# Polysketch attention and an ELU layer on one core: batch 1's attention output in products of 64 rows, its rows exchanged by DMA, and a new order around it

## The chip, the cores and the metric

The kernel runs on one core of a Trainium2 chip, and all seven inputs and the output lie in the chip's memory. The metric is the device time of one execution in microseconds (us), the lower the better. Engines are named as in the profile: PE is TensorE's matrix product and PEld its weight load, DVE is VectorE, ACT is ScalarE, POOL is GpSimd, and SP is the engine that here only issues DMA transfers. ACTq and SPq are the instructions with which ScalarE and SP issue transfers.

## The reference

Batch 4, 4 heads, sequence 1088, head dimension 32; the second part has 4352 tokens, 128 features and 2048 hidden units.

```
phi(x): a = S1 x, b = S2 x (8 values each); phi = outer(a, b), 64 features
kv  = sum over s of phi(k)[s, f] * v[s, d]         # per batch and head, 64 x 32
z   = sum over s of phi(k)[s, f]
att = (phi(q) kv) / (phi(q) z + 1e-6)              # seq x 32 per head
x   = att with the heads side by side              # 4352 x 128
h   = x @ w_in
g   = h if h > 0, else exp(min(h, 0)) - 1
out = g @ w_out
```

Inputs for q, k, v, the sketches S1, S2 and the two weight matrices are rounded to f32 on the chip where they come wider.

## The kernel before, in words

**Groups.** The 4352 tokens are worked in groups of 512 (numbers 0 to 7, two to a batch: groups 2 and 3 are batch 1, 4 and 5 batch 2, 6 and 7 batch 3) and one last group 8 of 256 that has the last 64 tokens of each batch. The hidden units are 8 column pairs `cp` of 2 x 128.

**The dense part of one group and one cp.** `mm1` (L910) makes h in two halves c, each 128 x 512 in a PSUM buffer named h, of which there are four; `elu_a` (L923) runs two ScalarE instructions (Relu, then Exp), `elu_d` (L934) one VectorE instruction that writes gg and frees the PSUM buffer; `sums7` (L791) forms on GpSimd, in three instructions, the sums that the seven-product scheme needs; `mm2_seven` (L819) adds seven block products of gg and of prepared weights (`weights7`, L783) into two accumulators in PSUM (pa and pb). At a group's end `fin_seven_copy`, `fin_seven_a`, `fin_seven_b`, `fin_seven_c` join the blocks and send the output rows by 16 transfers on SP's queue; `fin1` (L955) does so for group 0 with 8 transfers.

**The queries of a pair of groups.** `queries` (L751) takes two PSUM buffers named h and two named qps. With a group among its second argument it runs `q1` (L567), the sketch of the queries in products of 32 x 32; `q1_out` transposes the results, `q2_prod`, `q2_sum`, `q2_rec`, `q2_an` make the denominator and scale, `q2_half` (L694) forms the 64 features per token and head in two halves i, all on VectorE. `q4` (L702) brings the features onto the partitions, and `queries` with the group among its first argument makes the attention output x, which `q5_out` (ScalarE) copies to the tile xg that `mm1` reads.

**Two forms of the product for x.** A group named in `pairs` (L332: 4, 6 and 8) uses `q5_pairs` (L731): 16 products of 64 rows x 32 columns, in two rounds e, with the 64 features of a token on 64 partitions. VectorE's transpose works inside blocks of 32 partitions, so for these groups `q4` transposes into a tile qpF and then exchanges blocks of 32 partitions between the partitions by 8 DMA transfers per half i (two e, two u, two f), into `exch[i]` (L681), a part of the SBUF that held raw weights at the start. They go on SP's queue, but for two of group 4's half 0, on ScalarE's. A group not in `pairs`, before the change only group 2 (with 3), uses `q5` (L719): 32 products of 32 x 32, in two rounds f that add up in PSUM, straight from VectorE's transpose. Each product is two instructions in the profile.

**The key side.** `KF_late`, `KO_a`, `KO_b` and `KA` make phi(k) and kv of a batch, `Z` and `Z_share` its z. `KT_out` (L458) transposes kv and writes it to a scratch in memory (kvd), from which transfers on SP's queue read it back as the products want it: four copies into kvs for `q5` (batch 1 only), and into `kv2` (kvp in the profile) two halves f for each half of the partitions; the batches in `pair_b` fill both halves of the partitions, batch 1 before the change only its lower half, for group 8.

**What sets the order.** From L1297 on, the order is written out by hand, call by call, for all engines together. Each engine runs its own instructions in that order and waits by semaphores for what they need; nothing is moved between engines. A PSUM buffer or tile is taken again when its last reader is done. Up to `width[0] = 64` (L1620) the products of the dense part are made in blocks of 32 columns, after it in blocks of 64.

Of the kernel before, what the change touches and what calls it, by code (L numbers as in the profile page):

```python
# [29 lines left out]
def kernel(  # L30
# [24 lines left out]
    P = 128  # L55
# [646 lines left out]
    def q4(g, i=0):  # L702

        m = heads(g) * un[g]
        if g not in pairs:
            qpT[g, i] = work.tile([P, 4 * H, 2, 32], F32, name="qpT", tag="qpT", bufs=2)
            nc.vector.transpose(qpT[g, i][:, :m].rearrange("p m f s -> p (m f s)"),
                                qp.pop((g, i))[:, :m].rearrange("p m i j -> p (m i j)"))
            return
        t = work.tile([P, 2, 4 * H, 32], F32, name="qpF", tag="qpT", bufs=2)  # L710
        nc.vector.transpose(t[:, :, :m].rearrange("p f m s -> p m f s"),
                            qp.pop((g, i))[:, :m].rearrange("p m (f i) j -> p m f (i j)", f=2))
        to = qpT[g, i] = exch[i if g < NQ - 1 else 2]
        for e in range(2):
            for u in range(0, 4, 2):
                for f in range(2):
                    (nc.scalar if g == 4 and not i and e and f else nc.sync).dma_start(to[32 * (u + f):32 * (u + f) + 32, e, :m], t[32 * (u + e):32 * (u + e) + 32, f, :m])
# [579 lines left out]
    transp(kT, "k", 3, 9, NT)  # L1297
    queries((), (2,), (1, 4))
    mm1(1, 3, (0,))
    q1_out(2, (2,))  # L1300
    mm2(0, 7, True, (0,))
    q1_out(2, (1,))
    weights7(slice(4, 8), 0)
    elu_a(0, 7, 1, (1,))
    elu_d(0, 7, 1)
    q1_out(2, (3,))
    mm2(0, 7, True, (1,))
    mm1(1, 4, (1,))
    q1_out(2, (0,))
    q2_prod(2)  # L1310
    elu_a(1, 3, 0, (0,))
    elu_a(1, 3, 0, (1,))
    mm1(1, 3, (1,))
    elu_a(1, 3, 1, (0,))
    elu_d(1, 3, 0)
    fin1(0)
    q2_sum(2)
    sums7(1, 2, 1)
    weights7(slice(4, 8), 2)
    q2_rec(2)  # L1320
    elu_a(1, 4, 1, (0,))
    q2_an(2)
    mm1(1, 6, (1,))
    mm1(1, 4, (0,))
    elu_a(1, 3, 1, (1,))
    elu_d(1, 3, 1)
    elu_a(1, 4, 0, (0,))
    mm2_seven(1, 1, True, False)
    q2_half(2, 0)
    elu_a(1, 4, 0, (1,))  # L1330
    elu_d(1, 4, 0)
    weights7(slice(2, 4), 3)
    elu_a(1, 4, 1, (1,))
    elu_d(1, 4, 1)
    weights7(slice(2, 4), 2)
    weights7(slice(4, 8), 1)
    mm1(1, 6, (0,))
    elu_a(1, 6, 0, (0,))
    elu_a(1, 6, 1, (0,))
    elu_a(1, 6, 0, (1,))  # L1340
    elu_a(1, 6, 1, (1,))
    sums7(1, 2, 2)
    mm2_seven(1, 2, False, False)
    mm1(1, 5, (0,))
    mm1(1, 5, (1,))
    sums7(1, 3, 0)
    sums7(1, 3, 1)
    q2_half(2, 1)
    weights7(slice(4, 8), 3)
    elu_a(1, 5, 0, (0,))  # L1350
    elu_a(1, 5, 1, (0,))
    elu_a(1, 5, 1, (1,))
    elu_d(1, 6, 1)
    sums7(1, 3, 2)
    elu_d(1, 6, 0)
    sums7(1, 4, 0)
    weights7(slice(0, 1), 1)
    sums7(1, 4, 1)
    sums7(1, 4, 2)
    weights7(slice(0, 1), 3)  # L1360
    mm2_seven(1, 3, False, False)
    elu_a(1, 5, 0, (1,))
    q4(2, 0)
    elu_d(1, 5, 1)
    elu_d(1, 5, 0)
    sums7(1, 5, 0)
    mm1(1, 7, (1,))
    mm1(1, 7, (0,))
    sums7(1, 5, 1)
    sums7(1, 5, 2)  # L1370
    q4(2, 1)
    elu_a(1, 7, 0, (0,))
    elu_a(1, 7, 0, (1,))
    keep_last(0)
    sums7(1, 6, 0)
    sums7(1, 6, 1)
    mm2_seven(1, 4, False, False)
    queries((2,), (), (2, 0))
    elu_a(1, 7, 1, (0,))
    elu_a(1, 7, 1, (1,))  # L1380
    mm2_seven(1, 5, False, False)
    q5_out(2, 1, 1)
    q5_out(2, 0, 0)
    q5_out(2, 0, 1)
    mm1(2, 0, (0,))
    q5_out(2, 1, 0)
    elu_a(2, 0, 0, (0,))
    elu_a(2, 0, 0, (1,))
    elu_d(1, 7, 0)
    sums7(1, 6, 2)  # L1390
    elu_d(1, 7, 1)
    sums7(1, 7, 0)
    transp(kT, "k", 2, 9, NT)
    KF_late(2, None)
    KF_late(3, (2, 1))
    KF_late_out(3, 1)
    KF_late_out(2, 1)
    elu_d(2, 0, 0)
    KF_late_out(2, 0)
    KF_late_out(3, 0)  # L1400
    mm1(2, 0, (1,))
    keep_last(1)
    sums7(1, 7, 1)
    elu_a(2, 0, 1, (0,))
    elu_a(2, 0, 1, (1,))
    KO_a(2, 0)
    elu_d(2, 0, 1)
    mm2_seven(1, 6, False, False)
    mm1(2, 1, (1,))
    KO_b(2, 0)  # L1410
    sums7(1, 7, 2)
    mm2_seven(1, 7, False, True)
    elu_a(2, 1, 1, (0,))
    mm1(2, 1, (0,))
    sums7(2, 0, 0)
    KO_a(2, 1)
    fin_seven_copy(1)
    KO_b(2, 1)
    mm1(2, 2, (1,))
    mm1(2, 2, (0,))  # L1420
    KA(2, (0,))
    sums7(2, 0, 1)
    elu_a(2, 1, 1, (1,))
    elu_d(2, 1, 1)
    fin_seven_a(1, 3)
    fin_seven_a(1, 0)
    fin_seven_a(1, 1)
    fin_seven_b(1, 0)
    fin_seven_a(1, 2)
    elu_a(2, 1, 0, (0,))  # L1430
    elu_a(2, 1, 0, (1,))
    elu_d(2, 1, 0)
    sums7(2, 1, 0)
    KA(2, (1,))
# [12 lines left out]
    fin_seven_b(1, 1)
    elu_d(2, 2, 1)
    sums7(2, 2, 0)
    mm1(2, 3, (1,))  # L1450
    elu_a(2, 3, 0, (1,))
    elu_a(2, 3, 1, (0,))
    zls[2] = ZC(2, kv_ps[2])
    KO_b(3, 0)
    mm2_seven(2, 0, True, False)
    elu_d(2, 3, 0)
    elu_a(2, 3, 1, (1,))
    elu_d(2, 3, 1)
    KO_a(3, 1)
    KO_b(3, 1)  # L1460
    Z(2, kv_ps[2], zls[2])
    mm1(2, 4, (0,))
    mm1(2, 5, (0,))
    sums7(2, 1, 1)
    elu_a(2, 4, 1, (0,))
    sums7(2, 1, 2)
    mm2_seven(2, 1, False, False)
    elu_a(2, 5, 0, (0,))
    elu_a(2, 4, 0, (0,))
    elu_a(2, 4, 1, (1,))  # L1470
    elu_d(2, 4, 1)
    sums7(2, 2, 1)
    sums7(2, 2, 2)
    mm1(2, 5, (1,))
    elu_a(2, 4, 0, (1,))
    elu_a(2, 5, 0, (1,))
    mm2_seven(2, 2, False, False)
    transp(qT, "q", 2, 0, 9)
    sums7(2, 3, 0)
    elu_d(2, 4, 0)  # L1480
    Z_out(2, kv_ps[2])
    fin_seven_c(1)
    transp(qT, "q", 3, 0, 9)
    elu_a(2, 5, 1, (0,))
    mm1(2, 6, (0,))
    KA(3, (0,))
    elu_a(2, 5, 1, (1,))
    elu_d(2, 5, 1)
    transp(qT, "q", 2, 9, NT)
    mm1(3, 0, (0,))  # L1490
    KA(3, (1,))
    elu_a(3, 0, 0, (0,))
    elu_a(3, 0, 0, (1,))
    mm1(3, 0, (1,))
    elu_d(2, 5, 0)
    mm1(2, 6, (1,))
    sums7(2, 3, 1)
    zls[3] = ZC(3, kv_ps[3])
    sums7(2, 3, 2)
    mm2_seven(2, 3, False, False)  # L1500
    elu_a(3, 0, 1, (0,))
    KT_out(3)
    Z(3, kv_ps[3], zls[3])
    sums7(2, 4, 0)
    sums7(2, 4, 1)
    sums7(2, 5, 0)
    sums7(2, 5, 1)
    Z_share(2)
    sums7(2, 4, 2)
    mm2_seven(2, 4, False, False)  # L1510
    elu_a(3, 0, 1, (1,))
    elu_d(3, 0, 0)
    Z_out(3, kv_ps[3])
    elu_d(3, 0, 1)
    sums7(3, 0, 0)
    sums7(2, 5, 2)
    mm1(2, 7, (0,))
    elu_a(2, 6, 0, (0,))
    elu_a(2, 6, 1, (0,))
    elu_a(2, 6, 0, (1,))  # L1520
    elu_d(2, 6, 0)
    elu_a(2, 6, 1, (1,))
    elu_d(2, 6, 1)
    transp(qT, "q", 3, 9, NT)
    Z_share(3)
    mm1(2, 7, (1,))
    elu_a(2, 7, 0, (0,))
    mm2_seven(2, 5, False, False)
    elu_a(2, 7, 1, (0,))
    elu_a(2, 7, 0, (1,))  # L1530
    elu_d(2, 7, 0)
    sums7(2, 6, 0)
    queries((), (4, 8), (3, 1))
    mm1(3, 2, (1,))
    elu_a(2, 7, 1, (1,))
    elu_d(2, 7, 1)
    elu_a(3, 2, 1, (0,))
    q1_out(4, (3,))
    elu_a(3, 2, 1, (1,))
    sums7(2, 6, 1)  # L1540
    mm1(3, 2, (0,))
    sums7(2, 6, 2)
    sums7(2, 7, 0)
    sums7(2, 7, 1)
    q1_out(4, (2,))
    elu_a(3, 2, 0, (0,))
    elu_a(3, 2, 0, (1,))
    mm2_seven(2, 6, False, False)
    q1_out(4, (0,))
    q1_out(4, (1,))  # L1550
    q1_out(8, (2,))
    q2_prod(4)
    q1_out(8, (1,))
    mm1(3, 1, (1,))
    sums7(2, 7, 2)
    mm2_seven(2, 7, False, True)
    q1_out(8, (0,))
    q2_sum(4)
    q2_rec(4)
    elu_d(3, 2, 1)  # L1560
    q2_an(4)
    q2_a(4, 1)
    elu_a(3, 1, 1, (0,))
    elu_d(3, 2, 0)
    sums7(3, 2, 0)
    mm1(3, 1, (0,))
    q2_half(4, 1)
    elu_a(3, 1, 1, (1,))
    elu_d(3, 1, 1)
    mm1(3, 4, (0,))  # L1570
    q4(4, 1)
    elu_a(3, 1, 0, (0,))
    elu_a(3, 1, 0, (1,))
    elu_d(3, 1, 0)
    mm1(3, 3, (0,))
    fin_seven_copy(2)
    fin_seven_a(2, 1)
    elu_a(3, 3, 0, (0,))
    fin_seven_a(2, 0)
    fin_seven_b(2, 0)  # L1580
    sums7(3, 0, 1)
    sums7(3, 0, 2)
    fin_seven_b(2, 1)
    fin_seven_b(2, 2)
    elu_a(3, 3, 0, (1,))
    mm1(3, 3, (1,))
    q2_a(4, 0)
    q2_half(4, 0)
    elu_a(3, 4, 0, (0,))
    sums7(3, 2, 1)  # L1590
    mm1(3, 4, (1,))
    sums7(3, 1, 0)
    mm2_seven(3, 0, True, False)
    sums7(3, 1, 1)
    elu_a(3, 4, 0, (1,))
    elu_d(3, 4, 0)
    sums7(3, 1, 2)
    elu_a(3, 4, 1, (0,))
    elu_a(3, 4, 1, (1,))
    elu_a(3, 3, 1, (0,))  # L1600
    elu_a(3, 3, 1, (1,))
    q4(4, 0)
    sums7(3, 2, 2)
    mm2_seven(3, 1, False, False)
    mm2_seven(3, 2, False, False)
    mm1(3, 5, (1,))
    elu_d(3, 4, 1)
    sums7(3, 4, 0)
    elu_d(3, 3, 0)
    q1_out(8, (3,))  # L1610
    elu_d(3, 3, 1)
    sums7(3, 3, 0)
    elu_a(3, 5, 1, (0,))
    elu_a(3, 5, 1, (1,))
    mm1(3, 5, (0,))
    elu_a(3, 5, 0, (0,))
    elu_a(3, 5, 0, (1,))
    elu_d(3, 5, 1)
# [355 lines left out]
```

## Time and profile before

| what | value |
|---|---|
| median of 3 runs | 259.54 us (258.89 to 260.28) |
| the profiled execution | 260.47 us, of which its span is 258.3 us |
| granted TensorE clock, mean | 0.997 of full |
| transfers | 16.56 MB in 30907 packets, mean 64 GB/s |
| first product of the reordered stretch (L1298's q1) starts | 52.85 us |
| product of groups 2 and 3 (L1378) starts | 70.06 us |
| sketch of the queries of groups 4, 5 and 8 (L1533) starts | 104.62 us |
| product of groups 4 and 5 (L1630) starts | 125.53 us |

How to read it: the page gives the busy time of each engine and its share of the span; the chain of work that ended last follows the end of the kernel back through what released each step; the timeline lists one engine's instructions by start and duration. Starts of PE in the timeline lie a few hundredths before those in the chain, since a product overlaps the one before it; the chain's pieces add up without overlap. A DMA issue is an instruction of SPq or ACTq; the transfer lands later, and the view of a tile gives both times.

### The profile page before, as it was taken

How to read it: one execution, taken by the hardware profiler on the slowest of the kernel's cores; microseconds unless marked ns; L12 is line 12 of the kernel's file. 1: busy time of each engine (PE TensorE's matmuls, PEld its weight loads, DVE VectorE, ACT ScalarE, POOL GpSimd, SP SyncE). 2: the span in 40 equal slices, each digit the busy share in tenths (PEclk: the TensorE clock that was granted, in tenths of full speed). 3: DMA queues.
4: the chain of work that ended last, by engine and by line, in shares of the span. 5: the costliest groups of instructions: out<-in, count | busy, mean ns of one | idle time of the engine just before them, and what ended most of it. 6: DMA issues, size and time to landing. Idle time of an engine off the chain costs nothing.

```text
span 258.3 us, 9778 instructions
## 1 busy us (share of the span) xinstructions
PE 251.8 (97%) x4101; PEld 159.8 (62%) x4101; DVE 174.6 (68%) x342; ACT 182.0 (70%) x357; POOL 184.1 (71%) x236
## 2 busy tenths in 40 slices
PE   8789999999999999999999999999999999999994
PEld 7653333426666677657648466666766666667994
DVE  5898998898859875797658587743455445644651
ACT  2589887748757657676577877578677777777792
POOL 5433365698994978877858887987888888888310
PEclk9999999999999999999999999999999999999998
DMA  6999593313000011114102004312021100110021
GB/s 178 303 366 238 177 285 65 95 23 55 7 5 4 15 18 27 25 35 105 35 13 31 0 7 94 83 39 33 11 32 28 19 3 0 24 20 3 3 33 31
DMA packets 30907, 16.56 MB, mean 64 GB/s; under 512 B 22512, under 2 KB 28016, under 8 KB 30864
## 3 DMA queue, kind: packets, MB, share of 16 engines
q1 hardware_dynamic: 29904, 15.04, 24.4%
q10 hardware_dynamic: 896, 0.84, 1.3%
q8 instruction: 32, 0.52, 0.9%
q14 instruction: 11, 0.09, 0.1%
q0 software_dynamic: 64, 0.07, 0.1%
HBM read 11.21 MB, written 2.36 MB: 53 GB/s over the span
## 4 chain that ended last, share of the span: by engine, by line
PE 94%; DMA 3%; ACTq 1%; ACT 0%; issue 0%; DVE 0%; DVEq 0%
PE h L259 46%; PE pb L839 18%; PE pa L839 15%; PE o L259 5%; PE ol L259 3%; DMA v<-in_v_dram 3%; PE kv L453 1%; PE qtp L640 1%; PE h L738 1%; PE h L574 1%; PE pb L815 1%; PE xps L666 1%; PE kv L439 1%; PE kfps L366 1%; ACTq L81 0%; PE h L726 0%
## 5 line engine op out<-in xcount | busy, mean ns | idle before, releaser
L938 DVE SCALAR_TENSOR_TENSOR gg<-e,h 128x512 f32<-128x512 f32 x128 | 85.8, 682 | 60.9 <-ACT e L932 49.6
L259 PE MATMUL h<-xg,W 128*32 128x512 f32 (+2 forms) x768 | 121.7, 584 | 0.7 <-DVE xg L678 0.7
L930 ACT ACTIVATE e<-h 128x512 f32<-128x512 f32 x128 | 74.7, 591 | 51.3 <-PE h L259 49.7
L795 POOL TENSOR_TENSOR tt<-gg 128x512 f32<-128x512 f32 x55 | 71.5, 1301 | 25.9 <-DVE gg L938 23.2
L932 ACT ACTIVATE e<-e 128x512 f32<-128x512 f32 x128 | 79.3, 630 | 3.2
L259 PEld LDWEIGHTS h<-xg,W 128*32 128x32 f32 (+1 forms) x768 | 34.8, 119 | 44.5 <-issue 32.9
L800 POOL TENSOR_TENSOR tt<-tt,gg 128x256 f32<-128x256 f32 x55 | 41.8, 762 | 3.1
L802 POOL TENSOR_TENSOR tt<-gg,tt 128x256 f32<-128x256 f32 x55 | 40.5, 738 | 3.4
L839 PEld LDWEIGHTS pa<-gg,W 128*64 128x64 f32 (+1 forms) x528 | 25.7, 125 | 25.9 <-issue 25.6
L839 PE MATMUL pa<-gg,W 128*64 128x128 f32 (+1 forms) x528 | 32.4, 273 | 0.0
L839 PE MATMUL pb<-tt,SS 128*64 128x128 f32 (+1 forms) x472 | 29.5, 273 | 0.0
L145 POOL TENSOR_TENSOR W<-W,raw 128x256 uint32<-128x256 uint32 (+2 forms) x12 | 11.6, 977 | 20.3 <-ACT e L932 4.5
L839 PE MATMUL pa<-tt,SS 128*32 128x128 f32 (+1 forms) x404 | 25.3, 273 | 0.0
L839 PEld LDWEIGHTS pb<-tt,SS 128*64 128x64 f32 (+1 forms) x472 | 22.7, 127 | 0.0
L839 PE MATMUL pb<-tt,W 128*64 128x128 f32 (+1 forms) x292 | 21.9, 273 | 0.0
L839 PE MATMUL pb<-gg,SS 128*64 128x128 f32 (+1 forms) x292 | 21.8, 273 | 0.0
L839 PEld LDWEIGHTS pa<-tt,SS 128*32 128x32 f32 (+1 forms) x404 | 17.0, 120 | 0.0
L259 PE MATMUL o<-gg,W 128*32 128x512 f32 x128 | 15.3, 593 | 0.0
L839 PEld LDWEIGHTS pb<-gg,SS 128*64 128x64 f32 (+1 forms) x292 | 13.9, 124 | 0.0
L839 PEld LDWEIGHTS pb<-tt,W 128*64 128x64 f32 (+1 forms) x292 | 13.9, 124 | 0.0
L991 DVE SCALAR_TENSOR_TENSOR gg<-e,h 128x256 f32<-128x256 f32 x16 | 6.6, 418 | 6.4 <-PE h L259 3.2
L259 PEld LDWEIGHTS o<-gg,W 128*32 128x32 f32 x128 | 4.1, 110 | 9.3 <-issue 7.1
(181 smaller groups left out, 268.9 us busy)
## 6 DMA issues: line engine op xcount, KB each, us to landing
raw<-in_moe_w_in_dram SPq DMA_DIRECT2D x8, 256.0 KB, 6.6
raw<-in_moe_w_out_dram SPq DMA_DIRECT2D x8, 256.0 KB, 6.4
raw<-qpF SPq DMA_DIRECT2D x30, 64.0 KB, 2.0
out_dram<-ob SPq DMA_DIRECT2D x112, 16.0 KB, 1.5
hd_k<-in_k_dram SPq DMA_DIRECT2D x3, 544.0 KB, 8.7
hd_q<-in_q_dram SPq DMA_DIRECT2D x3, 544.0 KB, 8.3
v<-in_v_dram SPq DMA_DIRECT2D x4, 288.0 KB, 8.8
v<-in_v_dram SPq DMA_DIRECT2D x3, 256.0 KB, 8.8
```

The lines of the kernel that those rows point to most:

```text
L145: nc.gpsimd.tensor_tensor(dst.bitcast(U32), dst.bitcast(U32), words(raw)[0], op=ADD)
L259: nc.tensor.matmul(dst[c:c + tile], lhs[:, c:c + tile], rhs, skip_group_check=True, tile_position=(0, c), **kw)
L366: nc.tensor.matmul(ps[g2][32 * c:32 * c + 32, :32 * KT], Sxp[r].rearrange("p x c r -> p (x c r)"), kT[b][r, u * KT:u * KT + KT, 32 * w:32 ...
L439: nc.tensor.matmul(kv_ps[0][32 * h:32 * h + 32, :R * R], vt[0][:, (h * KT + i) * D:(h * KT + i + 1) * D], feats[0, i // 5][:, i % 5, h].re ...
L795: nc.gpsimd.tensor_tensor(_ap(ts[g, cp][:, 0], [[4 * P, 2], [P, 2], [1, P]]), _ap(gs[g, cp][:, 0, P:], [[4 * P, 2]] + us), _ap(gs[g, cp][: ...
L800: nc.gpsimd.tensor_tensor(t[:, 1], t[:, 2], quarter(g, cp, 0, 0), op=ADD)
L802: nc.gpsimd.tensor_tensor(t[:, 3], quarter(g, cp, 1, 0), t[:, 1], op=SUB)
L839: nc.tensor.matmul(bank[r:r + width[0], P * col:P * col + P], lhs[:, w:w + width[0]], rhs[:, u], start=(first and i in ((0,) if g == 1 els ...
L930: nc.scalar.activation(e, hs[g, cp][c][:, :n], RELU, scale=-1.0)
L932: nc.scalar.activation(e, e, EXP, scale=-1.0)
L938: nc.vector.scalar_tensor_tensor(gs[g, cp][:, c, :n], es[g, cp][:, c, :n], -1.0, hs[g, cp][c][:, :n], op0=ADD, op1=MAX)
L991: nc.vector.scalar_tensor_tensor(gs["last", k // 2][:, k % 2, :2 * P], es["last", k // 2][:, k % 2, :2 * P], -1.0, hs["last", k][:, :2 * P ...
```

## The change

Group 2 (with 3) is taken into `pairs`, so that batch 1's x is made by `q5_pairs` as the other batches' are; kvs has no batch left, and `KT_out(1)` reads kv back by four transfers in place of six. `q4(2, 0)` and `q4(2, 1)` each issue 8 transfers, of which those with e = 1 and f = 1, two per half, go on ScalarE's queue, the rest on SP's. The calls between the end of batch 3's first key transposes and `width[0] = 64` are the same as before, in another order; the calls before and after stand as they were.

```diff
-    pairs = (4, 6, 8)
+    pairs = (2, 4, 6, 8)
     pair_b = [g // 2 for g in pairs if g < 8]
-    kvs = {b: const.tile([P, H, 2, D], F32, name=f"kvs{b}") for b in (1, )}
+    kvs = {b: const.tile([P, H, 2, D], F32, name=f"kvs{b}") for b in ()}
...
-                    (nc.scalar if g == 4 and not i and e and f else nc.sync).dma_start(to[32 * (u + f):32 * (u + f) + 32, e, :m], t[32 * (u + e):32 * (u + e) + 32, f, :m])
+                    (nc.scalar if g == 2 and e and f or g == 4 and not i and e and f else nc.sync).dma_start(to[32 * (u + f):32 * (u + f) + 32, e, :m], t[32 * (u + e):32 * (u + e) + 32, f, :m])
```

The order around batch 1's product, cut to the calls that the text speaks of (each list in its own order; calls left out between them):

```
before                              after
queries((), (2,), (1, 4))           queries((), (2,), (1, 4))
mm1(1, 3, (0,))                     q1_out(2, (2,)), q1_out(2, (0,))
q1_out(2, ...) four times           mm2(0, 7, True, (0,))
elu_d(0, 7, 1)                      mm1(1, 3, (1,)); elu_d(0, 7, 1)
mm1(1, 4, (1,))                     q1_out(2, (1,)), q1_out(2, (3,)), q2_prod(2)
q2_prod(2)                          fin1(0); mm1(1, 3, (0,)); mm1(1, 4, (0, 1))
elu_d(1, 3, 0); fin1(0)             q2_sum, q2_rec, q2_an, q2_half(2, 0)
q2_sum, q2_rec, q2_an               mm2_seven(1, 1); mm2_seven(1, 2)
mm1(1, 6, (1,)); mm1(1, 4, (0,))    elu_d(1, 3, 1)
mm2_seven(1, 1)                     q4(2, 0)
q2_half(2, 0)                       elu_d(1, 3, 0), elu_d(1, 4, 1)
mm1(1, 6, (0,)); mm2_seven(1, 2)    mm1(1, 5, (1,)), mm1(1, 5, (0,))
mm1(1, 5, (0, 1)); q2_half(2, 1)    elu_d(1, 4, 0); q2_half(2, 1)
mm2_seven(1, 3)                     mm1(1, 6, (1,)), mm1(1, 6, (0,))
q4(2, 0)                            q4(2, 1)
elu_d(1, 5, 1), elu_d(1, 5, 0)      elu_d(1, 5, 0), elu_d(1, 5, 1)
mm1(1, 7, (1,)), mm1(1, 7, (0,))    mm2_seven(1, 3); elu_d(1, 6, 1), elu_d(1, 6, 0)
q4(2, 1)                            mm1(1, 7, (0,)), mm1(1, 7, (1,))
mm2_seven(1, 4)                     mm2_seven(1, 4); mm2_seven(1, 5)
queries((2,), (), (2, 0))           queries((2,), (), (2, 0))
```

And around the product of groups 4 and 5:

```
before                              after
queries((), (4, 8), (3, 1))         queries((), (4, 8), (3, 1))
...                                 ...
q2_half(4, 1); elu_d(3, 1, 1)       fin_seven_copy(2); q2_half(4, 1)
q4(4, 1)                            elu_d(3, 1, 1); q4(4, 1)
fin_seven_copy(2)                   fin_seven_a, fin_seven_b (2)
fin_seven_a, fin_seven_b (2)        q2_half(4, 0)
q2_half(4, 0)                       mm2_seven(3, 0); mm2_seven(3, 1)
mm2_seven(3, 0); elu_d(3, 4, 0)     elu_d(3, 4, 0), elu_d(3, 4, 1)
q4(4, 0)                            mm1(3, 5, (0,)), mm1(3, 5, (1,))
mm2_seven(3, 1); mm2_seven(3, 2)    q4(4, 0)
mm1(3, 5, (1,)); elu_d(3, 4, 1)     mm2_seven(3, 2)
mm1(3, 5, (0,)); mm1(3, 6, (1, 0))  mm1(3, 6, (1,)), mm1(3, 6, (0,))
mm2_seven(3, 3)                     mm2_seven(3, 3)
queries((4,), (6,), (3, 7))         queries((4,), (6,), (3, 7))
```

More of the change, by code (lines that the diff above doesn't have):

```diff
@@ L1308 @@
+    weights7(slice(4, 8), 3)
+    queries((), (2,), (1, 4))
+    q1_out(2, (2,))
+    q1_out(2, (0,))
+    elu_a(0, 7, 1, (1,))
+    mm2(0, 7, True, (0,))
+    mm1(1, 3, (1,))
+    elu_d(0, 7, 1)
+    mm2(0, 7, True, (1,))
+    elu_a(1, 3, 1, (0,))
+    weights7(slice(4, 8), 2)
+    q1_out(2, (1,))
+    q1_out(2, (3,))
+    q2_prod(2)
+    elu_a(1, 3, 1, (1,))
+    fin1(0)
+    mm1(1, 3, (0,))
+    mm1(1, 4, (0,))
     mm1(1, 4, (1,))
-    q1_out(2, (0,))
-    q2_prod(2)
     elu_a(1, 3, 0, (0,))
-    elu_a(1, 3, 0, (1,))
@@ L1336 @@
-    weights7(slice(4, 8), 1)
+    elu_a(1, 4, 0, (0,))
+    q2_sum(2)
+    q2_rec(2)
+    q2_an(2)
+    q2_half(2, 0)
+    mm2_seven(1, 1, True, False)
+    mm2_seven(1, 2, False, False)
+    elu_a(1, 3, 0, (1,))
+    elu_a(1, 4, 1, (0,))
+    elu_a(1, 4, 1, (1,))
+    elu_a(1, 4, 0, (1,))
+    elu_d(1, 3, 1)
+    q4(2, 0)
+    elu_d(1, 3, 0)
+    elu_d(1, 4, 1)
+    mm1(1, 5, (1,))
+    mm1(1, 5, (0,))
+    elu_a(1, 5, 0, (0,))
+    elu_a(1, 5, 0, (1,))
+    sums7(1, 3, 0)
+    sums7(1, 3, 1)
@@ L1337 @@
+    sums7(1, 3, 2)
+    elu_d(1, 4, 0)
+    sums7(1, 4, 0)
+    q2_half(2, 1)
+    mm1(1, 6, (1,))
     mm1(1, 6, (0,))
+    sums7(1, 4, 1)
+    elu_a(1, 5, 1, (0,))
+    elu_a(1, 5, 1, (1,))
     elu_a(1, 6, 0, (0,))
     elu_a(1, 6, 1, (0,))
[L1340 to L1350, printed above, removed]
@@ L1525 @@
+    elu_a(2, 7, 0, (1,))
+    elu_d(2, 7, 1)
+    elu_d(2, 7, 0)
     Z_share(3)
[L1526 to L1531, printed above, removed]
+    queries((), (4, 8), (3, 1))
+    q1_out(4, (2,))
     sums7(2, 6, 0)
[L1533 removed]
+    sums7(2, 6, 1)
+    sums7(2, 7, 0)
+    mm1(3, 2, (0,))
     mm1(3, 2, (1,))
[L1535 to L1538, printed above, removed]
```

381 lines of the change are left out of this document (178 added, 203 removed).

## The prediction, as it was put on record before the changed kernel ran

> **What bounds the kernel now.** I read three views in this order: the page's busy times, the chain of work that ended last, and the timeline of the queue that would carry the new transfers.
>
> ```profile
> span 258.3 us, 9778 instructions
> PE 251.8 (97%) x4101; PEld 159.8 (62%) x4101; DVE 174.6 (68%) x342; ACT 182.0 (70%) x357; POOL 184.1 (71%) x236
> ...
> PE 94%; DMA 3%; ACTq 1%; ACT 0%; issue 0%; DVE 0%; DVEq 0%
> ```
>
> TensorE is busy nearly all the time and makes up 94% of the chain; the other three engines have about 30% to spare each. So what TensorE saves is won, and what TensorE waits is lost for good. How much of its time is waiting? The change reorders everything from the query projection of groups 2 and 3 (L1298, starts at 52.92 in the chain) to the product of groups 4 and 5 (L1630, over at 127.35): 74.43 us. From the chain's pieces I add up what TensorE must do there: 40 halves of mm1 at 0.858 (34.3), 19 mm2_seven at 1.53 (29.1), two halves of mm2 (1.7), the key products of batches 2 and 3 (3.65) and the four query stages (0.65 + 1.43 + 1.16 + 1.74 = 4.98). That is 73.7. **Only 0.7 us of this stretch is gaps**, most of them 0.13 to 0.15 us where the array goes from 32-row products back to 128-row ones. A better order can win at most these 0.7 us.
>
> **The product itself.** The chain shows the old form and, for group 4, the form that batch 1 is to get:
>
> ```profile
> 69.91 0.22 PE pb L839 x8
> 70.13 0.34 PE h L726 x2
> ```
>
> ```profile
> 125.39 0.22 PE pb L839 x4
> 125.61 0.33 PE h L738
> 125.98 0.17 PE h L738
> 126.20 0.17 PE h L738
> 126.63 0.33 PE h L574 x2
> ```
>
> The old form (L726, 64 instructions of 32 rows) runs from 70.13 to the next unit at 71.56, 1.43 us. The 64-row form (L738, 32 instructions) runs from 125.61 to 126.63, 1.02 us. Saved: **0.41 us**. The bounds: the other use of L738, at 176.1, takes 0.89 before its next part (0.54 saved); if the return to 128 rows costs the new form another 0.12, 0.29.
>
> **The transfers.** For this form a VectorE transpose is not enough: q4 must also move 32-partition blocks across partitions by DMA, 8 per half, 16 in all, 12 on SP's queue and 4 on ScalarE's. What such a transfer costs is seen in group 4's:
>
> ```profile
> L717 SPq DMA_DIRECT2D raw<-qpF x30: 507/589/1713, 113.4 to 164.6; - x30
> ...
> L717 ACTq DMA_DIRECT2D raw<-qpF x2: 598/730/863, 118.9 to 119.6; - x2
> ...
> DMA to landing us min/median/max: 1.8/2.0/4.3
> ```
>
> These are the lines of the tile qpF: durations of one issue in ns (least, median, most), and the time to landing. The timeline of SP's queue has group 4's transfers, and what the queue does at the time of batch 1's product:
>
> ```profile
> 56.32 1.73 SPq L465 DMA_DIRECT2D kvs<-kvd  x4
> 58.09 0.91 SPq L469 DMA_DIRECT2D kvp<-kvd  x2
> 59.09 4.91 SPq L965 DMA_DIRECT2D out_dram<-ob  x8
> ...
> 113.37 11.06 SPq L717 DMA_DIRECT2D raw<-qpF  x14
> ```
>
> SP starts one such transfer every 0.64 us, and now and then one holds the queue for 1.7 (117.18 and 121.51); 3 of the 38 take over 1.3. Each lands 2.0 us after its start. Group 4's second set shows the whole path: VectorE's transpose ends at 118.91, SP is still busy with the first set until 119.63, its six run to 124.44, the last one starts at 123.85 and lands at 125.85. TensorE begins the product at 125.53 and the second half of it (e = 1, which needs that transfer) at 125.97. So 6.6 us from transpose to product were enough **with 0.1 us to spare**. That is the measure for the new order.
>
> **Batch 1 in the new order.** TensorE: without waits the product comes one mm2_seven later than now (five instead of four stand ahead of it), at 70.13 + 1.53 = 71.66, its e = 1 half at 72.1. VectorE: up to the elu that ends at 55.09 its list is as before; then, by the start-to-start times of the same rows (0.37 and 0.4 for two q1_out, 0.89 for the product, 0.63 fin1, 0.44, 0.39, 0.40 for sum, reciprocal and scaling, 1.14 for each q2_half, 0.60 for an elu, 1.18 for each transpose), q4's first half ends at 61.5 and the second at 65.7. VectorE has no pause there, but 6 us before the product. SP: four copies of kv for batch 1 in place of six, from 56.32 to 58.09; the 8 output rows of fin1(0), whose transpose is over by then, 4.95, to 63.05; six transfers at 0.64 to 66.9; six more to 70.75. The last starts at 70.1 and lands at **72.1, just when it is needed**. So nothing lies behind a free queue here: one long issue among these twelve (3 in 38 gives about one) puts 1.1 us before the product. I take 0.5, bounds 0 and 1.1. ScalarE's four issues (0.73 each) cost nothing: the first two wait for the transpose that ends at 61.5, when ScalarE would otherwise wait for mm1(1, 5), ready at about 63.7; the second two come at 67.4 and push two exps to about 70, ahead of the product that needs their PSUM. If that cover fails, 1.5 us are queued in front of these exps and of all sums of cp 6, and reach TensorE at most by 1 us.
>
> **Groups 4 and 5 in the new order.** The TensorE work between their query projection and their product is the same, 20.9 us. But on VectorE the order now puts elu_d(3, 4, 1) ahead of q4(4, 0), and elu_d(3, 1, 1) waits for an exp behind fin_seven_copy(2), which waits for the end of mm2_seven(2, 7). By the same start-to-start times q4(4, 0) ends 15.6 us after the projection starts, against 14.3 now (118.91 less 104.62). The 6.6 us become 5.3. SP's backlog in front of it shrinks from 0.7 to between 0 and 0.5. Without a long issue the e = 1 transfers are in time to about 0.1; with one, as before had at 121.51, they are 1.1 late. I take 0.4, bounds 0 and 1.1.
>
> All else in the stretch moves without being added. GpSimd's and ScalarE's lists, summed the same way, reach each mm2_seven's sums and each mm1's PSUM buffer in time, often by a few tenths only; I cost it at 0, and it hides behind the 30% that these engines have free.
>
> **The sum**: -0.41 + 0.5 + 0.4 = +0.5 us. It is made against the profiled execution, 260.47 us (258.3 span and 2.2 around it), which lies 0.9 above the median of the runs, 259.54. Carried to the median: **260.0 us**.
>
> **Rivals.**
> 1. *The transfers are in time* (no long issue falls on the twelve and the six): -0.4, 259.1. For it: at the plain 0.64 and 2.0 both sets land on the moment. Against it: 3 in 38 issues are long, and two of them fell on group 4's 14.
> 2. *SP's queue becomes the bound of both products* (slower). TensorE reaches each product before the last transfer lands. Its price: 1.1 per long issue, and up to 1.8 where a landing takes 3.8 instead of 2.0. In the trace SP's transfers that started beside ScalarE's (119.63 to 120.86) landed after 2.0, 3.8 and 3.3 us, ScalarE's after 2.3 and 4.3, while those that ran alone took 2.0 to 2.1. Both products late by 1.1 to 1.8 each, less 0.4: 261.3 to 262.7. It decides from 1.7 us of waiting in all, where 0.41 is repaid and 1.3 are lost.
>    The Trainium skill says in "DMA: Bandwidth & Descriptors", section "Issuing engines are not separate DMA queues", that transfers started by different engines run on the same 16 DMA engines and interleave, so that a second issuing engine only saves issue time. The longer landings agree with it; by that rule ScalarE's share shortens SP's line by 2 issues a half, yet stretches the landings it was to speed up.
> 3. *VectorE's unbroken list is late* between 55 and 68: mm1(1, 5) and mm1(1, 7) wait for PSUM that its elus free. Each 0.6 us elu of lateness comes out of TensorE once: 261 and more.
> 4. *The order also closes the gaps*: -0.41 - 0.7 = -1.1, 258.4; only if every switch between row sizes got cheaper, which no row shows.
>
> **Chances.** Forecast (some waiting, the sum between -0.4 and +1.3) 0.50; rival 1, 0.17; rival 2, 0.23; rival 3, 0.06; rival 4, 0.04. The measurement of this kernel tells about 0.5% (1.3 us) from no change. The forecast and rival 1 lie within: 0.67. Rivals 2 and 3 are slower: 0.29. Faster: 0.04. The range runs from rival 1 less 0.2 to the middle of rival 2: 258.9 to 261.7.
>
> **What would show it.** In the changed profile L726 is gone and L738 has 32 instructions more; the product of groups 2 and 3 should take about 1.0 us, starting at 71.7 if nothing waits. A wait of it for DMA, with SP's queue busy without pause from 58 to 71, shows rival 2 or the half of it that the forecast holds; no wait there shows rival 1. For groups 4 and 5, compare the end of q4(4, 0)'s transpose with the start of the product: 5.3 us. Waits of mm1 for DVE between 60 and 70 show rival 3. I am wrong altogether if TensorE waits over 1 us somewhere that has neither a transfer nor a PSUM buffer behind it.

## The result, and the profile after

| | before | after |
|---|---|---|
| median, runs taken side by side (22 each) | 260.01 us | 261.41 us |
| profiled execution | 260.47 us | 260.42 us |
| its span | 258.3 us | 258.5 us |

The ratio of the times is 1.005, with a 95% interval of 1.0035 to 1.0064: slower by 0.9 to 1.7 us, best 1.3. The forecast was 260.0 for the median then known, 259.54, so +0.5. The two spans differ by only 0.2 us, but that is chance: the reordered stretch began at 52.85 us in the profile of before and at 51.15 in that of after, and this start lies anywhere between 51.15 and 54.56 in the profiles below, with the same instructions ahead of it on TensorE. So all profiles below are compared **by stages**, from the first query product of groups 2 and 3 (L574) on.

The page of after, its busy times and the shares of the chain that ended last:

```profile
span 258.5 us, 9747 instructions
PE 252.8 (98%) x4069; PEld 159.3 (62%) x4069; DVE 175.5 (68%) x342; ACT 182.3 (71%) x357; POOL 183.9 (71%) x236
...
PE 90%; SPq 5%; DVE 2%; DMA 1%; issue 1%; ACT 0%; DVEq 0%
```

The 32 products that PE has less (4069 for 4101) are the form's, 64 become 32. SP's queue, which was not among the chain's shares before, now holds 5% of it: some 13 us of that chain are issues of transfers. The busy time of PE went up although it does less, since the trace counts most of a wait inside a run of products as busy (below, a group of 24 lasts 1.00 for 0.84 of work). Stage times show more (us; "wait-free" is what the stage takes with nothing waiting, from before's rows; for the product from group 4's in before, and for the way to the product of groups 4 and 5 from after's):

| stage | before | after | wait-free |
|---|---|---|---|
| first query product to the product for x of groups 2, 3 | 17.21, and 18.74 with mm2_seven(1, 5), which stands behind that product in before | 19.86 | 18.74 |
| that product | 1.43 (old form) | 2.21 | 1.03 |
| its end to the projection of groups 4, 5, 8 | 33.13, and 31.60 without mm2_seven(1, 5) | 31.61 | 31.60 |
| projection to the product of groups 4, 5 | 20.91 | 20.86 | 20.86 |
| that product and the projection behind it | 1.75 | 1.78 | 1.75 |
| the whole stretch | 74.43 | 76.32 | 73.98 |
| from there to the end of the span | 131.0 | 131.1 | |

Two rows carry the whole loss against the last column: 1.1 us **ahead of** the product, 1.2 us **in** it. The timeline of TensorE in after shows both (start, duration, line, operation, and in brackets the idle time and what ended it):

```profile
68.62 0.40 PE L839 MATMUL pa<-gg,W 128*32 128x128 f32 x8
...
69.28 1.00 PE L839 MATMUL pa<-tt,SS 128*32 128x128 f32 x24
70.66 0.43 PE L839 MATMUL pb<-tt,W 128*32 128x128 f32 x8 [0.38 <-POOL tt L802]
71.01 0.40 PE L738 MATMUL h<-raw,kvp 64*32 64x256 f32 x1
...
72.13 0.38 PE L738 MATMUL h<-raw,kvp 64*32 64x256 f32 x1
72.66 0.37 PE L738 MATMUL qps<-raw,kvp 64*32 64x256 f32 x1 [0.16 <-DMA raw<-qpF]
...
73.22 0.42 PE L839 MATMUL pa<-gg,W 128*32 128x128 f32 x8
```

mm2_seven(1, 5) runs from 68.62 to 71.01, 2.39 us for 1.53 of work: its last products wait for a sum from GpSimd (tt, L802). mm2_seven(1, 3) before it had taken 1.88. Then the product starts, and its second round stands still from 72.13 to 72.66 for a transfer. In the chain that ended last, the transfers' side reads (start, duration, what):

```profile
59.59 1.92 SPq L965
...
62.35 0.60 SPq L717
...
66.92 1.64 SPq L717
...
69.87 0.59 SPq L717
...
70.50 2.03 DMA raw<-qpF
...
72.66 0.37 PE qps L738
```

Nothing but SP's own instructions stands in this chain from 56.69 to 70.46: the eight output rows of fin1(0) (L965, one of them 1.92 us in place of 0.45), then the twelve transfers of the exchange (L717, one of 1.64 in place of 0.59), then the landing. VectorE's two transposes had ended at 59.83 and 64.73, long before their last transfers were issued.

For groups 4 and 5 nothing waited. The timeline of VectorE has the second transpose:

```profile
118.31 1.24 DVE L711 STREAM_TRANSPOSE qpF<-qp 128x1024 f32<-128x1024 f32 x1
```

It ends at 119.55, the product starts at 125.76: 6.2 us, not the 5.3 of the prediction. SP's 14 issues took 9.53 us, the longest of them 1.08, for 11.06 in before, where two took 1.71 and 1.66.

### The profile page after: what moved, and what is told of

It reads as the page before. It is cut to its first block, busy times and chain, and to the rows that moved or that the text cites. A ratio compares the mean times of both kernels' runs of the same rounds, so it can differ in the third digit from the quotient of the medians.

```text
span 258.5 us, 9747 instructions
## 1 busy us (share of the span) xinstructions
PE 252.8 (98%) x4069; PEld 159.3 (62%) x4069; DVE 175.5 (68%) x342; ACT 182.3 (71%) x357; POOL 183.9 (71%) x236
## 4 chain that ended last, share of the span: by engine, by line
PE 90%; SPq 5%; DVE 2%; DMA 1%; issue 1%; ACT 0%; DVEq 0%
PE h L259 42%; PE pb L839 17%; PE pa L839 13%; PE o L259 5%; SPq L717 3%; PE ol L259 3%; SPq L965 2%; PE idle L267 1%; PE kv L453 1%; PE qtp L640 1%; PE h L738 1%; DMA raw<-qpF 1%; PE h L574 1%; PE pb L815 1%; DVE abw L589 1%
## 5 line engine op out<-in xcount | busy, mean ns | idle before, releaser
L795 POOL TENSOR_TENSOR tt<-gg 128x512 f32<-128x512 f32 x55 | 70.5, 1281 | 27.7 <-DVE gg L938 19.4
L800 POOL TENSOR_TENSOR tt<-tt,gg 128x256 f32<-128x256 f32 x55 | 42.0, 764 | 3.3
L802 POOL TENSOR_TENSOR tt<-gg,tt 128x256 f32<-128x256 f32 x55 | 40.1, 733 | 3.5
```

Source lines behind the costliest of these rows:

```text
L795: nc.gpsimd.tensor_tensor(_ap(ts[g, cp][:, 0], [[4 * P, 2], [P, 2], [1, P]]), _ap(gs[g, cp][:, 0, P:], [[4 * P, 2]] + us), _ap(gs[g, cp][: ...
L800: nc.gpsimd.tensor_tensor(t[:, 1], t[:, 2], quarter(g, cp, 0, 0), op=ADD)
L802: nc.gpsimd.tensor_tensor(t[:, 3], quarter(g, cp, 1, 0), t[:, 1], op=SUB)
```

## The experiments

All twelve were timed against the kernel before in runs side by side. The table gives the ratio of times with its interval and the stages of each one's own profile; each line is told below.

| run | ratio to before | to the product | product | the 33 us behind it | group 4's product | stretch |
|---|---|---|---|---|---|---|
| before | 1 | 18.74 (with mm2_seven(1, 5)) | 1.43 | 31.60 | 1.75 | 74.43 |
| after | 1.005 (1.0035 to 1.0064) | 19.86 | 2.21 | 31.61 | 1.78 | 76.32 |
| e1_rows_later | 1.005 (1.0031 to 1.007) | 19.85 | 1.43 | 31.61 | 1.75 | 75.50 |
| e2_pool_later | 1.0068 (1.0049 to 1.0087) | 19.79 | 1.58 | 32.29 | 2.03 | 76.55 |
| e3_both | 1.0068 (1.0048 to 1.0089) | 19.78 | 1.46 | 32.42 | 1.75 | 76.28 |
| e4_no_exchange | 1.0035 (1.0016 to 1.0055) | 19.83 | 1.03 | 31.85 | 1.75 | 75.32 |
| e5_old_form | 1.0034 (1.0011 to 1.0057) | 19.88 | 1.43 | 31.61 | 2.23 | 76.01 |
| e6_old_order | 1.026 (1.0222 to 1.0298) | 17.65 | 7.42 | 33.77 | 1.75 | 81.60 |
| e7_sums_early | 1.0003 (0.9984 to 1.0022) | 18.93 | 1.57 | 31.61 | 1.75 | 74.72 |
| e8_sums_early_rows_later | 0.9991 (0.997 to 1.0011) | 18.91 | 1.79 | 31.61 | 2.44 | 75.61 |
| e9_sums_early_old_form | 0.9998 (0.9984 to 1.0012) | 18.91 | 1.42 | 31.73 | 2.61 | 75.54 |
| e10_sums_early_no_exchange | 0.9998 (0.9978 to 1.0017) | 18.92 | 1.03 | 31.78 | 1.75 | 74.34 |
| e11_sums_early_half_on_scalar | 1.0054 (1.0029 to 1.0079) | 19.93 | 1.14 | 32.33 | 1.75 | 76.01 |
| e12_elu_first_alone | 1.0052 (1.0033 to 1.0071) | 19.88 | 1.56 | 31.61 | 1.86 | 75.77 |

(A stage comes from one profiled execution, a ratio from 4 to 14 executions, after's from 22. Group 4's product varies by up to 0.9 from one profile to the next, so ratio and stretch need not agree in every line. In e6 mm2_seven(1, 5) is behind the product, as in before.)

### Is it SP's queue, GpSimd's list, or the order?

**e1_rows_later** sends fin1(0)'s eight output rows (L965) behind batch 1's exchange, so SP is free for the exchange when the first transpose ends. It starts the exchange 8.7 us after the first query product, in after 11.2.

```diff
+    def fin1_out(g):
+        ob = obs.pop(g)
...
     q4(2, 1)
+    fin1_out(0)
```

> The changed kernel, with group 0's 8 output transfers issued on SP's queue behind batch 1's exchange instead of ahead of it; all else as it is. The stretch from the first query product to the end of groups 4 and 5's product took 74.5 us before and 76.3 in the changed kernel. Theory A (SP's queue sets when batch 1's product can end): q4's first transfers start when the transpose ends, the last lands 1.3 to 2.5 us earlier, the product takes 1.0 to 1.2 us in place of 2.2: stretch about 75.2, ratio to before about 1.002. Theory B (GpSimd's late sums set it, the transfers are a remainder): the product still waits for little, but the 1.2 us in front of it stay; the same 75.2. Rival C (the transfers are slow for another reason, landing or ScalarE's share): no gain, 76.3.

The product did go down, from 2.21 to 1.43, and the other wait, ahead of the product, stayed (19.85). The ratio did not move. With the same transfers as after the product took 1.58 and 1.56 in e2 and e12, so 2.21 may be more than most executions of after have; stages of executions without a profile are not known. SP's queue alone was not the cause. And 1.43 is not 1.03, although the last transfer here was issued at 70.55, landed 2.1 later and TensorE only came to its round at 72.9. What was left shows in the rows of L738 in the profile of e1, between 66 and 75 us, beside those of e4 (the same stretch with no exchange at all):

```profile
L738 PEldq EVENT_SEMAPHORE  x9: 51/51/51, 72.0 to 73.1; - x9
```

```profile
L738 PEldq EVENT_SEMAPHORE  x4: 51/51/51, 71.5 to 71.9; - x4
```

A semaphore wait takes TensorE's weight-load queue 51 ns even if what it waits for is there already. Nine of them belong to the product in e1, and six of these come behind its first weight load; in after ten and seven, in e4 four and one. In e4's timeline eight products start within 0.05 us of one another; in e1's the starts come in ones to fives, 0.1 apart. In before's group 4 four of the six waits were over ahead of time (from 124.4 on, for a product at 125.5). In e1 TensorE had just stood still for GpSimd, its queue had no lead, and most waits fell among the products. e11 below has nine waits too, but only four of them behind the first weight load, and takes 1.14. This is read from the rows: no run takes the waits away and leaves the transfers.

**e2_pool_later** moves the four GpSimd calls that the new order has early (`keep_last(1)`, `keep_last(0)`, `weights7(slice(0, 1), 1)`, `Z_share(0)`) behind `sums7(1, 5, 2)`, ahead of which they had pushed the sums of cp 3 to 5.

```diff
-    keep_last(1)
...
-    keep_last(0)
-    weights7(slice(0, 1), 1)
-    Z_share(0)
...
     sums7(1, 5, 2)
+    keep_last(1)
+    keep_last(0)
+    weights7(slice(0, 1), 1)
+    Z_share(0)
```

> The changed kernel, with four GpSimd calls that nothing needs before 80 us (both keep_last, weights7 of the first cp, Z_share of batch 0) moved behind sums7(1, 5, 2). They take 1.4 us in all, 2.4 where VectorE slows one. Theory A: mm2_seven(1, 3) and (1, 5) no longer wait for sums (1.2 us won ahead of the product), but the last transfer still lands at the same time, so the wait moves into the product: it begins near 69.8 and takes about 3.3; stretch 76.3, ratio 1.005 as the changed kernel has. Theory B: the 1.2 us are won: 75.1, ratio 1.000 to 1.002.

It won nothing, 19.79, and lost 0.7 behind the product, where the moved calls now delay the sums of cp 6. The timeline of GpSimd and the chain that ended last in e2 say why:

```profile
62.02 1.29 POOL L795 TENSOR_TENSOR tt<-gg 128x512 f32<-128x512 f32 x1 [1.12 <-DVE gg L938]
```

```profile
60.13 1.23 DVE qpF L711
61.37 0.59 DVE gg L938
...
62.02 1.30 POOL tt L795
...
70.81 0.73 POOL tt L802
```

GpSimd was now free earlier, and idle for 1.12 us: the first sum, of cp 3, needs elu_d(1, 3, 0), which the new order puts on VectorE *behind* q4(2, 0)'s transpose (L711). From there nine instructions of GpSimd run without a pause to 71.5. So two causes lie one behind the other in the same row, and each hides the other.

**e3_both** is e1 and e2 together.

> Both edits together: group 0's output transfers behind the exchange, and the four GpSimd calls behind sums7(1, 5, 2). Theory A and B both: neither wait is left, or a few tenths of the transfers' (the last one lands between 70.0 and 71.2 on the changed kernel's scale, the e = 1 half is due at 70.2): stretch 74.0 to 75.0, ratio 0.998 to 1.002. Theory A says that this gain is more than the sum of the two single ones; theory B that it is just their sum.

1.0068: both theories fell as they stood. **e4_no_exchange** leaves out batch 1's 16 transfers; x of groups 2 and 3 is made from what lies in that SBUF.

```diff
-        for e in range(2):
+        for e in range(2 if g > 2 else 0):
```

> The changed kernel without batch 1's 16 exchange transfers (x of groups 2 and 3 is then made from what lies in that SBUF). Theory A: the product waits for nothing, 1.0 to 1.1 us in place of 2.2; GpSimd's lateness ahead of it stays and shows: stretch 75.1 to 75.3, ratio about 1.002, the same as with the output transfers moved. Theory B: the same. If SP's and ScalarE's issues also slow something else (ScalarE's exps behind its four issues, group 4's transfers), it is lower than that.

With no transfer to wait for, the product takes 1.03, the form's promise to the hundredth, and the kernel is still 0.35% slower. That 0.9 us is not the exchange's.

### The order against the form

**e5_old_form** keeps the new order but has the 32-row form for batch 1, its copies of kv and no exchange; **e6_old_order** keeps before's order with the new form and its exchange (four of its transfers on ScalarE's queue).

```diff
-    pairs = (2, 4, 6, 8)
+    pairs = (4, 6, 8)
...
-    kvs = {b: const.tile([P, H, 2, D], F32, name=f"kvs{b}") for b in ()}
+    kvs = {b: const.tile([P, H, 2, D], F32, name=f"kvs{b}") for b in (1, )}
```

> The new order with the old form of batch 1's product: group 2 out of pairs again, kvs copied again, no exchange. It shows what the order alone does. Theory C (the new order puts mm2_seven(1, 5) ahead of the product, and its sums are the last of nine on GpSimd that start only after elu_d(1, 3, 0), behind q4's transpose): the product starts 19.8 us after the first query product, as in the changed kernel, against 18.74 without waits, and takes its 1.43; stretch 75.4 to 75.7, ratio 1.003 to 1.005. Theory A (only the transfers are late): 74.4 and ratio 1.000.

> The new form in the old order: pairs and kvs as in the change, the calls as before. q4's second half ends about 16.3 us after the first query product and the product is due at 17.2. Theory A and C both: SP is busy with group 0's rows until about 11.1, then 12 transfers at 0.64 and one or two long ones, the last lands near 23 to 24.5; the product's e = 1 half is due at 17.7, so it ends 5 to 6.5 us late; stretch 79.5 to 81, ratio 1.019 to 1.025.

The order by itself costs 1.1 us ahead of the product (19.88) and 0.34% in time, with the old form as with the new. The form by itself, in the old order, costs 7 us. Its product waits four times in TensorE's timeline, the longest time 2.01 us:

```profile
73.47 0.59 PE L738 MATMUL h<-raw,kvp 64*32 64x256 f32 x2 [2.01 <-DMA raw<-qpF]
```

That has a price that was not expected, in the view by windows of e6 (window, busy time of PE, PEld, DVE, ACT, POOL, granted clock of TensorE, DMA):

```profile
69.00:73.00 4.00, 1.33 (x13) 0.31 (x8) 1.58 (x3) 2.34 (x4) 3.77 (x6) 1.00 0.64 145
73.00:74.50 1.50, 0.59 (x2) 0.14 (x2) 0.42 (x1) 0.00 (x0) 1.42 (x3) 1.00 0.43 98
74.50:77.00 2.50, 2.31 (x26) 0.83 (x30) 0.00 (x0) 0.00 (x0) 2.32 (x4) 0.57 0.20 46
77.00:80.00 3.00, 3.00 (x64) 2.12 (x64) 0.00 (x0) 1.20 (x4) 0.00 (x0) 0.79 0.03 5
```

In the 5.5 us from 69.0 to 74.5 TensorE was busy for 1.9; then its granted clock was 0.57 for 2.5 us and 0.79 for 3. By estimate that is 2.5 x 0.43 + 3 x 0.21 = 1.7 us on top of the waiting, and brings the 5 to 6.5 of the expectation to the 7.2 that the stretch gained. The Trainium skill, "TensorE: Matmul & The Clock Gate", section "Part 1: The HAM clock gate", says that an array that was idle for a window of some 3.4 us is clocked at half speed until it has been busy for one. The half speed and its length agree by an estimate from the two windows: 1.7 us lost at half speed are 3.4 us of it. But no 3.4 us of e6 were idle throughout (3.6 us of idling in pieces, the longest 2.01), and no run here shows how much idling is enough. In after, where TensorE idled 0.5 us between 69 and 73, the clock stayed at 1.00.

**e7_sums_early** removes both causes that e2 showed: elu_d(1, 3, 0) goes ahead of q4(2, 0), and the four GpSimd calls go behind `sums7(1, 7, 1)`, where GpSimd has a pause. **e8_sums_early_rows_later** adds e1's edit.

```diff
     elu_d(1, 3, 1)
-    q4(2, 0)
     elu_d(1, 3, 0)
+    q4(2, 0)
...
     sums7(1, 7, 1)
+    keep_last(1)
+    keep_last(0)
+    weights7(slice(0, 1), 1)
+    Z_share(0)
```

> The changed kernel with elu_d(1, 3, 0) ahead of q4(2, 0) on VectorE, and the four GpSimd calls that are not needed yet moved behind sums7(1, 7, 1), where GpSimd waits for 5.7 us. Theory C: GpSimd starts the sums of cp 3 about 1 us earlier, mm2_seven(1, 5) waits for nothing, the product starts at 18.7 to 19.0 in place of 19.86. But the last transfer lands no earlier (21.4), so the product takes about 3: stretch 76 to 76.5, ratio 1.004 to 1.006, no gain by itself. Theory B (the sums alone): stretch 75.2.

> The same two edits, and group 0's 8 output transfers issued behind batch 1's exchange. Theory C: both chains are shortened, GpSimd's by 1 us and SP's by 1.3 or more: product starts at 18.7 to 19.0, last landing 19.0 (no long issue) to 20.2, so that it takes 1.1 to 2.0; stretch 74.0 to 75.2, ratio 0.997 to 1.002, the first version that need not be slower than the kernel before.

With both causes gone the product comes after 18.93, and the kernel takes the time of before. The expectation had named no gain, because the last transfer would land at 21.4 us after the first query product as in after, and the product would take about 3. It landed at 19.8, and the product took 1.57: in this profile SP was done with group 0's rows at 8.1, in after's at 11.1. That profile is of e7's fastest execution (259.26 us, the median is 260.25), so the 1.57 says less than the ratio. The pairs without transfers are free of this: e4 and e5 with late sums take 1.0035 and 1.0034, e10 and e9 below with early sums 0.9998 and 0.9998, about 0.9 us each time; within each pair the intervals just meet, those of after and e7 lie apart. The chain that ended last in e7 shows no gap and no transfer between the last mm2_seven and the product:

```profile
69.71 0.66 PE pa L839 x24
70.37 0.22 PE pb L839 x8
70.59 0.33 PE h L738
```

e8 got no further: with the elu first, q4(2, 0)'s transpose ends 9.8 us after the first query product and not 8.7 (0.6 for the elu, the rest for operations that ran slower beside GpSimd's), and from there twelve issues and a landing set the end, whether SP was free before or not.

### What is left for the form

**e9** is e7 with e5's edit, **e10** is e7 with e4's (x again from what lies in the SBUF). **e11** gives ScalarE's queue all eight transfers with e = 1. **e12** is the changed kernel with elu_d(1, 3, 0) first, and nothing else.

```diff
-(nc.scalar if g == 2 and e and f or g == 4 and not i and e and f else nc.sync)
+(nc.scalar if g == 2 and e or g == 4 and not i and e and f else nc.sync)
```

> The repaired order of the run with the sums early (one elu ahead of q4(2, 0), four GpSimd calls behind sums7(1, 7, 1)), with the 32-row product form and no exchange. If the order is now right, its stretch is 18.9 to the product + 1.43 + 31.6 + 22.6 = 74.55 us, 0.1 from the kernel before, ratio 1.000. Theory 'the form repays itself only where the exchange is hidden': the new form in the same order took 1.57 there (74.72), so the two are equal within 0.2 us. Rival 'the form is a gain and something else eats it': 0.4 us slower than the new form, ratio 1.002.

> The repaired order with the new form but without batch 1's 16 transfers (x of groups 2 and 3 is made from what lies in that SBUF). This is the floor of the new form: product in 1.03 us, stretch 18.9 + 1.03 + 31.6 + 22.6 = 74.15, 0.3 below the kernel before and 0.55 below the same order with transfers: ratio 0.998 to 0.999. If ratio is 1.000 or above, the order still loses somewhere that the stages don't show.

> The repaired order with all 8 transfers of round e = 1 on ScalarE's queue in place of 4, so SP has 8 instead of 12. Theory 'SP's queue sets the last landing': its line gets 2.5 us shorter, the product finds all landed and takes 1.1 to 1.4; stretch 74.3, ratio 0.998 to 0.999. Rival 'ScalarE's queue pays for it': four more issues at 0.55 to 0.75 push the exps of cp 5 and 6 back by 1.5 to 3 us; their sums come last on GpSimd, so the product starts 0.5 to 1.5 later and the ratio is 1.002 to 1.005.

> The changed kernel with elu_d(1, 3, 0) ahead of q4(2, 0), and nothing else. Theory 'two causes in one row': GpSimd is busy with its four early calls until 61.1 anyway, so the elu alone wins nothing, q1 to product stays 19.8, as it did when only the GpSimd calls were moved; and q4(2, 0) is 0.6 later, so the product waits as long or longer: ratio 1.005 to 1.007. Rival 'the elu alone is the cause': q1 to product 18.9 to 19.2, ratio 1.001 to 1.003.

In the repaired order, new form, new form without transfers, and old form measure 1.0003, 0.9998 and 0.9998. The stages say 1.57, 1.03 and 1.42 for the product; 0.4 us is 0.15% of the time, and the intervals are 0.15 to 0.2% to either side. So the form has nothing left that a measurement of this kernel can tell, and in the profiles the exchange gives back what the form saves.

e11 is the rival's case. The exchange was in time (product 1.14), but the first four issues hold ScalarE's queue for 2.82 us, and in ScalarE's and TensorE's timelines that comes out as a wait for PSUM:

```profile
61.70 2.82 ACTq L717 DMA_DIRECT2D raw<-qpF  x4
```

```profile
66.65 2.16 PE L259 MATMUL h<-xg,W 128*32 128x512 f32 x16 [0.74 <-DVE gg L938]
```

mm1(1, 7) waits 0.74 for an elu whose exps were queued behind the transfers; the product comes 1.0 later, and another 0.7 goes behind it. e12 gave 19.88, as its first theory had it (its product took 1.56 only, where the theory had 2.2 or more): with GpSimd busy until 62.88 in its profile, an earlier elu is worth nothing. Only the two edits together win the 0.9 us ahead of the product.

In e9 group 4's product took 2.61, and the chain leads to SP's queue:

```profile
123.64 1.75 SPq L717
...
126.71 2.04 DMA raw<-qpF
...
128.79 0.40 PE qps L738
```

Two of SP's 14 issues took 1.70 and 1.75 us in place of 0.59, as two did in before. Over the twelve profiles with the new order around groups 4 and 5 this stage is above 1.75 by 0.03, 0.28, 0.48, 0.69, 0.86 and 0.11 in six and by nothing in the other six: 0.2 on average.

The long issues are not scattered over the list. Of group 4's fourteen, one of the sixth to eighth took over 0.95 us in all fourteen profiles, and one of the eleventh to fourteenth in twelve of them. Of batch 1's twelve, one of the eighth to tenth took 1.45 to 2.06 us in all seven profiles of the new order that have twelve. So the exchange met one long issue each time, and a sum should take it whole (1.1) and not by half. Why it is long stays open; no run was made for it.

No version beat both kernels: the lowest ratio, e8's 0.9991 (0.997 to 1.0011), can't be told from 1.

## Why the prediction came out as it did, point by point

**The form (-0.41).** Right: 1.43 in e5 and 1.03 in e4, -0.40.

**Transfers of batch 1 (+0.5, bounds 0 and 1.1).** Right mechanism: in after SP's queue and its long issues, not the transposes, set the last landing, which the prediction had at 19.2 us after the first query product and which came at 21.4. Of the 2.2 us, 1.0 stood ahead of the exchange (fin1's rows began 0.3 later and took 5.60 us for 4.95; each of the two figures has one long issue in it, 1.92 and 1.53) and 1.2 in it, by the one long issue that was allowed for. In after's profile the product took 1.18 over its 1.03; in e2 and e12, with the same transfers, 0.55 and 0.53. The mean, 0.75, is within the bounds, but in all three the late sums had given the transfers 1.1 us more; in e7, without them, it was 0.54. Missing from the step was a part that is no landing at all: 0.1 to 0.4 us that go with semaphore waits of 51 ns (1.14 and 1.43 with all or nearly all landed in time, against 1.03), which group 4's rows had not shown since TensorE came to them with a lead. ScalarE's four issues cost nothing ahead of the product, as said: without them it came after 19.83 (e4), with them after 19.86.

One reading in rival 2 does not hold. It puts landings of 3.3 and 3.8 us down to ScalarE's transfers beside them and says that those that ran alone took 2.0 to 2.1. In before the transfer that SP issued at 115.92, 3 us ahead of ScalarE's first, landed after 3.64; in e9 those of 117.78 and 118.41, 3 us ahead of ScalarE's too, landed after 3.63 and 3.16. Each time a long issue of SP follows (117.18, 119.05). So the late landings go with the long issues, and the trace does not show that ScalarE's share stretched them. Rival 2, SP's queue as the bound of *both* products, did not happen.

**Groups 4 and 5 (+0.4, bounds 0 and 1.1).** Too large, 0 in after and 0.2 on average. The step had q4(4, 0) 5.3 us ahead of the product because elu_d(3, 1, 1) would wait for an exp behind fin_seven_copy(2). In after VectorE did not wait for it; the transpose ended 6.2 us ahead. What remains are SP's long issues, which it named.

**"All else in the stretch moves without being added ... I cost it at 0."** This is the step that failed: it was **1.1 us**, the largest term of all. The list of GpSimd was said to reach each mm2_seven's sums "in time, often by a few tenths only", and to hide "behind the 30% that these engines have free". A share of free time over the whole span hides nothing at one place. The order takes mm2_seven(1, 5) ahead of the product, so its sums, the last of nine, are due there; and it has put a copy, a preparation of weights and z's share ahead of these nine, and a transpose ahead of the elu that the first of them needs. GpSimd's timeline in after:

```profile
56.95 1.23 POOL L515 COPY qE<-qT 128x64 f32<-128x64 f32 x1
...
61.08 1.28 POOL L795 TENSOR_TENSOR tt<-gg 128x512 f32<-128x512 f32 x1
62.44 1.60 POOL L800 TENSOR_TENSOR tt<-tt,gg 128x256 f32<-128x256 f32 x1
...
69.87 0.73 POOL L802 TENSOR_TENSOR tt<-gg,tt 128x256 f32<-128x256 f32 x1
```

And the two q2_half in VectorE's timeline beside them, which took 1.22 each in before:

```profile
56.78 1.30 DVE L699 TENSOR_TENSOR qp<-an,abw 128x1024 f32<-128x1024 f32 x1
...
61.53 1.92 DVE L699 TENSOR_TENSOR qp<-an,abw 128x1024 f32<-128x1024 f32 x1
```

Three times (1.29 + 0.74 + 0.73) with their gaps are 8.6 us from 61.08, and 0.9 more for an L800 that takes 1.60 beside VectorE's q2_half in place of 0.74: over at 70.60. TensorE would have used that last sum at 18.74 - 0.22 us after the first query product, 69.67. By these rows the product is 0.93 late, and 1.1 were measured. To take away the calls alone (e2) or the elu's place alone (e12) wins nothing; both together (e7) win 0.9. The prediction named its own end for this: "wrong altogether if TensorE waits over 1 us somewhere that has neither a transfer nor a PSUM buffer behind it". Taken over the two units that wait for sums it did: mm2_seven(1, 3) took 0.35 and mm2_seven(1, 5) 0.86 over 1.53. So the number was near for reasons that were in part others.

**The sum by what was measured**: -0.4 (form) + 1.1 (GpSimd's sums) + 0.75 (exchange) + 0.2 (groups 4, 5) = +1.65 us, against 1.3 measured (0.9 to 1.7). Forecast were -0.41 + 0 + 0.5 + 0.4. The four terms come from different profiles and lean on each other (a later product leaves the transfers more time), so the sum is rough. The median, 261.4, lies inside the forecast's range of 258.9 to 261.7, and at the very edge of 0.5%. In part that is luck: the range was drawn for waits on transfers, and a term that had been put at nothing filled most of it. The upper end is also not the middle of rival 2's 261.3 to 262.7 as stated, which would be 262.0.

**Rivals 3 and 4.** TensorE's timeline in after has no mm1 that waits for VectorE between 60 and 70, so rival 3 did not come as described. But VectorE's list did matter, by the elu behind q4's transpose that GpSimd's first sum waits for. Rival 4 did not come: the stages where nothing waits take what they took before (31.61 for 31.60).

**Why a large change moved so little.** e6 and e5 split it: the form in the old order loses 7 us, because its exchange needs 6 to 8 us between the last transpose and the last landing (6.4 in e7, 7.7 in e6). The new order makes that room, and wins nearly all of it back; it pays 1.1 us for it with sums that are late. Repaired (e7), the whole is worth nothing, since the 0.4 of the form goes to the exchange.

## What to carry to other kernels

When an order is changed, sum the list of *every* engine up to the instruction that the bound engine will wait for, and compare with the moment at which that engine wants it; a small margin ("a few tenths") is a cost, not a zero. If a repair of one suspected cause wins nothing, look at the chain again before dropping it: two causes in a row hide each other (ahead of the product e2 and e12 alone win 0 to 0.1 us, e7 together 0.9). And a form that is cheaper on the bound engine but needs transfers is worth its saving less their waits: here 0.40 against 0.1 to 1.2.

## What the runs showed of the hardware that was not expected

- A wait on a semaphore that is set already takes TensorE's weight-load queue 51 ns. Waits ahead of a product did not lengthen it (before's group 4: four of six ahead, 1.02 us). With six among the products, and all or nearly all transfers landed, one took 1.43 (e1), with four 1.14 (e11), with one 1.03 (e4); no run isolates the waits.
- One issue in about fourteen of the exchanges on SP's queue takes 1.1 to 2.1 us in place of 0.59 (46 of 636 over the fourteen profiles), and within one place or two it is the same one of the list each time: 1.64 in after, 1.96 in e1, 1.70 and 1.75 in e9. Transfers issued just ahead of it land after 2.6 to 4.1 us in place of 2.0 (before, after, e5, e9).
- VectorE's operations that read two tiles of SBUF and GpSimd's operations beside them slow each other: GpSimd's L800 takes 1.60 in place of 0.74 beside q2_half, a copy 1.23 in place of 0.23, and q2_half itself 1.92 in place of 1.22. The Trainium skill has this in "SBUF — State Buffer", section "Who interferes with whom", as a port pair that the two share and that one of them holds for a whole instruction; a loss of 0.9 to 1.0 us, near to the length of one such instruction, agrees with it.
- After 3.6 us of idling in pieces within 5.5, TensorE's granted clock was 0.57 over the next 2.5 us and 0.79 over 3 more (e6).
